# Twelve groups of relayout transfers, handed to the queue three feeds earlier

## The chip, the core and the metric

The kernel runs on one core of a Trainium2 chip. The metric is the device time of one execution in microseconds (us). The engines are TensorE (PE; its weight loads stand apart as PEld), VectorE (DVE), ScalarE (ACT), GpSimd (POOL) and SyncE (SP). SP computes nothing here: it issues most of the DMA transfers, one after the other, from one queue.

## The reference

An RWKV-like recurrence over 768 steps runs for 4 batches of 8 heads of width 40. Its outputs, put side by side per token (3072 tokens of 320 numbers), go through a two-layer feed-forward block with a gate.

```python
for t in range(S):
    y[:, :, t] = np.einsum('bhd,bhde->bhe', rt, state)
    Sa = np.einsum('bhde,bhe->bhd', state, at)
    state_decay = state * wt[:, :, None, :] - np.einsum('bhd,bhe->bhde', Sa, bt)
    state = state_decay + np.einsum('bhd,bhe->bhde', vt, kt)
...
x = np.ascontiguousarray(attn_out.transpose(0, 2, 1, 3)).reshape(B * S, H * D)
h = x @ w_in                       # 320 -> 2048
g = np.where(pos, h, np.where(neg, 0.0, (h + beta) ** 2 / (4.0 * beta)))
return (g @ w_out).astype(np.float32)   # 2048 -> 320
```

## The kernel before, in words

The recurrence is worked in 24 chunks of 32 steps. What a chunk needs is prepared for sets of four chunks at a time, in the background: `prelude` loads w, a, k and b of the next 8 steps from memory (`ld_w`, `ld_a`, `ld_k`, `ld_b`, L258), and ACT copies `ld_w` into the tile `wz` (L267) for two scans on DVE (L235); POOL multiplies (L280, L290, L299) and the rows go out to a scratch tensor (L250). `ab_set` loads rows back from scratch into `lw` and `tiab` (L317); ACT shifts them (L323), DVE transposes them into `ea` (L338) and PE multiplies (L349). `invert` works a triangular inverse on POOL (L376, L382). The chunk itself is `chain`: matmuls L532, L542, L558, L569, L598 with evictions on ACT (L553, L563) and DVE (L576, L600) in between.

A chunk's output lands in the tile `Y` in two roundings: ACT writes the high part (L588) and POOL the low part (L589). Each time two chunks are complete, 64 steps of 4 batches (a token group, 256 columns) are there. `relayout` then copies them by six transfers on SP (L618 three times, L624 twice, L627 once) from `Y` into one of two tiles `X`. The feed-forward block of that group, `moe`, reads `X` in its first matmuls (`ph<-X,w`, L650), gates on ACT, DVE and POOL (L660 to L667) and multiplies again (`po<-w,gh` and `po<-w,gl`, L681). `weights` converts the two weight matrices, in the background too.

All of this is written into one program order, and each engine takes its own instructions in that order. A chunk has four steps; at each, one stage of two chains is written, and then `fill` writes six feeds. A feed (`feed`) writes so many matmuls of `moe` as stand for 1280 columns, then some weight conversion, then `background` some rows of `prelude`, `ab_set` and `invert`. So the transfers that the background issues on SP stand between the six feeds. At the end of the second step of every even chunk, behind the whole fill, stands `relayout`. The feed-forward of a group begins six feeds (7680 columns) behind its relayout: for the first group by the value of `owed`, for the others because a group's work is as many columns as the feeds of two chunks.

A transfer on SP waits for semaphores of the data that it reads and writes. The six of a group wait for the last POOL rounding of `Y` (L589); the matmuls L650 wait for the six; the next roundings of `Y` wait for them too.

Of the kernel before, what the change touches and what calls it, by code (L numbers as in the profile page):

```python
# [44 lines left out]
TRAIL = 2.5  # L45
# [10 lines left out]
def rwkv_moe_kernel(ctx: ExitStack, tc: tile.TileContext, r, k, v, w, a, b, w_in, w_out, ident_d, mask_d, out):  # L56
# [328 lines left out]
    def adopt(s):  # L385

        drain("inv", s)
        W = lw[:, 1024:2048]
        nc.vector.transpose(tinv.rearrange("p c h i -> p i (c h)"), W.rearrange("p (a i) -> p i a", i=32))
        turned_out.add(s)  # L390
# [33 lines left out]
    def background(n):  # L424

        due = []
        for key in ("inv", "ab", "rows"):
            for s in range(1, NS):
                a, b = window(key, s)
                if a < n <= b:  # L430
                    drain(key, s - 1)
                    at = spent.setdefault((key, s), [0])
                    due.append((key, s, at, size[key] * (gone(n) - gone(a)) / (gone(b) - gone(a))))
        while True:
            due = [(k, s, at, to) for k, s, at, to in due if done[k] < s and at[0] < to]
            if not due:
                return
            key, _, at, _ = max(due, key=lambda x: x[3] - x[2][0])
            at[0] += next(back[key])
# [3 lines left out]
    def load_ti(c, hb):  # L443
        drain("rows", c // 4)
        tis[c, hb] = tih[hb]
        load_rows(tih[hb], c, 0, 200, 16 * hb, 16)

    def load_cg(c, hb):
        cg = cgs[(2 * c + hb) % 3]
        hsel = slice(16 * hb, 16 * hb + 16)  # L450
        drain("rows", c // 4)
        sc = scr4[c // 4][c % 4][hsel]
        for f in range(2):
            vr, ur = 64 * (1 - f), 64 * (1 - f) + 32
            nc.sync.dma_start(
                cg[vr : vr + 32, f::2, C_S : C_S + 80], sc[f::2, :, O_V : O_V + 80].rearrange("h t x -> t h x")
            )
            nc.sync.dma_start(
                cg[ur : ur + 32, f::2, C_G : C_G + D], sc[f::2, :, O_B : O_B + D].rearrange("h t x -> t h x")
            )  # L460
# [6 lines left out]
    def shift(c, hb):  # L467
        shift_rows(tis[c, hb])

    def turn(c, hb, part):  # L470
        u = 2 * c + hb
        cg, pr = cgs[u % 3], prs[u % 3]
        t5 = tis[c, hb].rearrange("p h (j x) -> p h j x", x=40)[:, :, :, 0:32]
        if part == 0:
            for f in range(2):
                rows = slice(64 * f, 64 * f + 64)
                nc.vector.transpose(cg[rows, f::2, C_X : C_X + 32], t5[rows, :, 4, :])
        elif part == 1:
            evs[u] = work.tile([128, 8, 2, 32], F32, tag="ev", name="ev")
            nc.vector.transpose(evs[u], t5[:, :, 1:3, :])  # L480
        else:
            nc.vector.transpose(pr[:, :, :, 8:40], t5[:, :, 0:4:3, :])

    def scores(c, hb, parts=(0, 1)):
        u = 2 * c + hb
        for part in parts:
            (score_products, score_masks)[part](u)
# [119 lines left out]
    groups = [(t, 64) for t in range(0, S, 64)]  # L607

    def relayout(g):

        t0, nt = groups[g]
        if g < 2:
            Xt[g] = x_tile(g, F32R)
        X = flat(Xt[g % 2])[0:120, 0 : 24 * nt].rearrange("p (c n) -> p c n", c=6)
        Xb = X.bitcast(F32)
        yf = Y[0].bitcast(F32)[:, :, :, :, t0 % 64 : t0 % 64 + nt]
        for i, (f, p) in enumerate(((0, 0), (1, 0), (0, 2))):
            nc.sync.dma_start(  # L618
                Xb[40 * i : 40 * i + 40, 0:4, :].rearrange("e c (b t) -> e (c b) t", b=NB),
                yf[64 * f : 64 * f + D, p : p + 2].rearrange("e p j b t -> e (p j b) t"),  # L620
            )
        lo = Xb[:, 4:6, :].rearrange("e q (b t) -> e q b t", b=NB)
        for i in range(2):
            nc.sync.dma_start(  # L624
                lo[40 * i : 40 * i + 40], yf[64 : 64 + D, 2 + i, 0].unsqueeze(1).broadcast_to([D, 2, NB, nt])
            )
        nc.sync.dma_start(lo[80:120], yf[64 : 64 + D, 2:4, 1])  # L627
        return X
# [3 lines left out]
    Xs = {}  # L632
# [175 lines left out]
    def pull(gen, n=1):  # L808
        for _ in range(n):
            if next(gen, "end") == "end":  # L810
                return False
        return True
# [50 lines left out]
    def stage(c, hb):  # L863

        if (c, hb) in gens:
            next(gens[c, hb], 0)

    def finish_rounds():

        for f in rounds:  # L870
            f()
        rounds.clear()
# [31 lines left out]
    owed, idle = [0], [True]  # L904
# [7 lines left out]
    def feed(cols):  # L912

        if not Xs:
            return
        owed[0] += cols * (not idle[0])
        while owed[0] > 0:
            d = next(mgen)
            owed[0] = 0 if d is None else owed[0] - d
            idle[0] = d is None  # L920

    def catch_up():

        for f in deferred:
            f()
        deferred.clear()

    def fill():

        catch_up()  # L930
        for k in range(6):
            feed(1280)
            if first:
                first.pop(0)()
            due[0] += PACE
            while due[0] > 0:
                pull(wgen)
                due[0] -= 1
            background(now[0] + 10 / SLOTS * (k + 1) / 6)
        now[0] += 10 / SLOTS  # L940

    for c in range(NC + 1):
        nxt = c + 1 < NC
        if c < NC:
            if c:
                gens[c, 0] = chain(c, 0)
            gens[c, 1] = chain(c, 1)
        stage(c - 1, 1)
        if c:
            stage(c, 0)  # L950
        finish_rounds()
        if c < NC:
            if c and c % 4 == 0:
                adopt(c // 4)
            for j in (0, 1) if c else (2, 0, 1):
                turn(c, 1, j)
        fill()
        stage(c - 1, 1)
        stage(c, 0)
        if nxt:  # L960
            shift(c + 1, 0)
        finish_rounds()
        if c < NC:
            scores(c, 1)
        if nxt:
            load_ti(c + 1, 1)
        if nxt:
            load_cg(c + 1, 0)
            turn(c + 1, 0, 2)
        fill()  # L970
        for g, (t0, nt) in enumerate(groups):
            if t0 + nt == 32 * c:
                Xs[g] = relayout(g)
                if idle[0]:
                    owed[0], idle[0] = -TRAIL * 3072, False
        if c == NC:
            break
        stage(c, 0)
        stage(c, 1)
        finish_rounds()  # L980
        if nxt:
            for j in (0, 1):
                turn(c + 1, 0, j)
        fill()
        stage(c, 0)
        stage(c, 1)
        if nxt:
            shift(c + 1, 1)
        finish_rounds()
        if c + 2 < NC:  # L990
            load_ti(c + 2, 0)
        if nxt:
            scores(c + 1, 0)
            load_cg(c + 1, 1)
            turn(c + 1, 1, 2)
        fill()
# [33 lines left out]
```

## Time and profile before

| | |
|---|---|
| time, median of 3 runs | 774.89 us (773.26 to 779.03) |
| the profiled execution | 778.53 us, of it 776.8 us from its first to its last instruction (the span) |
| busy share of the span: PE, DVE, ACT, POOL | 87%, 76%, 61%, 56% |
| mean granted clock of TensorE | 0.916 of full speed |
| moved by DMA | 102.35 MB, 132 GB/s on the mean |

All starts below are us from the span's first instruction. An engine's row names its line, operation and tiles (`X<-Y`: writes X, reads Y); in square brackets stands how long the engine idled before it and what ended that. Rows of SP are transfers being issued; the length is that of the issue, not of the transfer.

### The profile page before, as it was taken

The numbers are of one execution on the slowest core, as the hardware profiler recorded it, in microseconds if no ns is written. First come the engines' busy times: TensorE is split into PE (matmuls) and PEld (weight loads), VectorE is DVE, ScalarE is ACT, GpSimd is POOL, SyncE is SP. The second block draws the span as 40 slices with busy tenths as digits, with TensorE's granted clock in tenths as the row PEclk, the third lists the DMA queues.
The fourth block names the chain that finished last, engine by engine and source line by source line (L and its number), as shares of the span: only waits on it lengthen the run. The fifth ranks groups of instructions, "written<-read, shape, count | busy, mean of one in ns | idle before, by whom it ended". The sixth has DMA issues, their size and how long they took to land.

```text
span 776.8 us, 35626 instructions
## 1 busy us (share of the span) xinstructions
PE 672.8 (87%) x15360; PEld 620.9 (80%) x15360; DVE 589.2 (76%) x1361; ACT 472.4 (61%) x1016; POOL 433.2 (56%) x603
## 2 busy tenths in 40 slices
PE   4546656796889889899988999999999999999997
PEld 4445546685779778789988889999999999999997
DVE  6999998887769678897788977788777786776211
ACT  5646756775566565565666566665665665655544
POOL 1232999765336998367576486563666732322332
PEclk9865656999699999999999999999999999999999
DMA  8898996998587758684558683443424234330100
GB/s 296 210 218 174 229 204 171 221 211 182 123 183 161 171 133 172 144 191 89 124 115 173 143 171 71 109 80 62 116 47 110 54 71 108 55 89 20 36 20 18
DMA packets 207084, 102.35 MB, mean 132 GB/s; under 512 B 153688, under 2 KB 200792, under 8 KB 206928
## 3 DMA queue, kind: packets, MB, share of 16 engines
q1 hardware_dynamic: 204336, 93.36, 54.2%
q0 software_dynamic: 2432, 6.56, 3.7%
q8 instruction: 121, 1.98, 1.1%
q14 instruction: 35, 0.29, 0.1%
q10 hardware_dynamic: 160, 0.16, 0.1%
HBM read 70.88 MB, written 27.53 MB: 127 GB/s over the span
## 4 chain that ended last, share of the span: by engine, by line
PE 54%; DVE 6%; POOL 4%; DMA 3%; ACT 2%; issue 2%; SPq 2%; POOLq 0%; ACTq 0%; DVEq 0%
PE ph L650 18%; PE po L681 17%; PE p L569 4%; PE p L558 3%; PE p L598 3%; PE p L498 2%; PE p L542 2%; PE p L532 2%; PE p L349 1%; DMA X<-Y 1%; POOL lw L382 1%; POOL lw L376 1%; POOL gl L667 1%; DVE gt L663 1%; DVE wz L235 1%
## 5 line engine op out<-in xcount | busy, mean ns | idle before, releaser
L650 PE MATMUL ph<-X,w 120*128 120x256 f32 x1536 | 219.7, 296 | 6.3 <-DMA X<-Y 5.8
L667 POOL TENSOR_TENSOR gl<-gt,gh 128x512 fp32r<-128x512 f32 x95 | 121.6, 1280 | 162.3 <-ACT gh L666 155.8
L650 PEld LDWEIGHTS ph<-X,w 120*128 120x128 f32 x1536 | 198.0, 198 | 13.9 <-issue 6.0
L681 PE MATMUL po<-w,gh 128*128 128x320 f32 x768 | 136.6, 320 | 4.6 <-ACT gh L666 3.8
L663 DVE SCALAR_TENSOR_TENSOR gt<-gt,ph 128x512 f32<-128x512 f32 x95 | 65.0, 684 | 85.2 <-ACT gt L661 72.8
L681 PEld LDWEIGHTS po<-w,gh 128*128 128x128 f32 x768 | 119.5, 197 | 6.7 <-ACT gh L666 5.0
L666 ACT CAST gh<-gt 128x512 fp32r<-128x512 f32 x95 | 58.8, 619 | 91.7 <-DVE gt L663 84.8
L660 ACT ACTIVATE gt<-ph,half_c 128x512 f32<-128x512 f32 x95 | 65.3, 687 | 54.5 <-PE ph L650 53.7
L382 POOL TENSOR_TENSOR lw<-lw 128x31 f32<-128x31 f32 (+15 forms) x155 | 86.9, 561 | 8.3
L376 POOL TENSOR_TENSOR lw<-lw 128x31 f32<-128x31 f32 (+15 forms) x155 | 85.5, 551 | 8.1
L576 DVE SCALAR_TENSOR_TENSOR cg<-p,pr 40x160 f32<-40x160 f32 x184 | 59.2, 322 | 34.6 <-PE p L569 32.5
L681 PE MATMUL po<-w,gl 128*128 128x320 f32 x384 | 75.8, 320 | 9.5 <-POOL gl L667 9.5
L510 DVE TENSOR_TENSOR cg<-p,mask 32x256 f32<-32x256 f32 x192 | 80.6, 420 | 3.6
L553 ACT ACTIVATE cg<-p 32x160 f32<-32x160 f32 x192 | 56.6, 295 | 30.6 <-DVE cg L549 16.3
L681 PEld LDWEIGHTS po<-w,gl 128*128 128x128 f32 x384 | 62.3, 195 | 11.6 <-POOL gl L667 11.3
L569 PE MATMUL p<-cg 128*64 128x72 f32 (+1 forms) x1536 | 64.0, 241 | 0.0
L549 DVE SCALAR_TENSOR_TENSOR cg<-p,mask 32x128 f32<-32x128 f32 x192 | 55.3, 288 | 11.0 <-ACT cg L553 5.8
L589 POOL TENSOR_TENSOR Y<-yt,Y 128x256 fp32r<-128x256 f32 x48 | 35.7, 744 | 48.5 <-ACT Y L588 48.4
L661 ACT ACTIVATE gt<-gt 128x512 f32<-128x512 f32 x95 | 60.0, 632 | 3.0
L569 PEld LDWEIGHTS p<-cg 128*64 128x64 f32 x1536 | 58.4, 150 | 0.4 <-issue 0.4
L558 PEld LDWEIGHTS p<-cg 128*40 128x40 f32 x1472 | 36.4, 131 | 21.2 <-ACT cg L553 13.1
L558 PE MATMUL p<-cg 128*40 128x40 f32 x1472 | 42.6, 219 | 12.2 <-ACT cg L553 12.2
(105 smaller groups left out, 1085.1 us busy)
## 6 DMA issues: line engine op xcount, KB each, us to landing
ti<-scr SPq DMA_DIRECT2D x96, 200.0 KB
cg<-scr SPq DMA_DIRECT2D x96, 80.0 KB
scr<-arena SPq DMA_DIRECT2D x16, 480.0 KB
X<-Y SPq DMA_DIRECT2D x36, 160.0 KB
scr<-wide SPq DMA_DIRECT2D x8, 640.0 KB
w<-in_moe_w_out_dram SPq DMA_DIRECT2D x16, 320.0 KB
tiab<-scr SPq DMA_DIRECT2D x28, 160.0 KB
cg<-scr SPq DMA_DIRECT2D x96, 40.0 KB
```

What stands on the lines that cost most here:

```text
L376: eng.tensor_mul(t3, W3[:, 0:n, j : j + 1].broadcast_to([128, n, m]), L3[:, j + 1 :, j].unsqueeze(1).broadcast_to([128, n, m]),)
L382: eng.tensor_sub(W3[:, 0:n, j + 1 :], W3[:, 0:n, j + 1 :], t3)
L510: nc.vector.tensor_tensor(out=cg[q, f::2, C_X : C_X + 64][:, 4 * i : 4 * i + 4].rearrange("p h (j x) -> p h j x", x=32), in0=ps[quarter(f, ...
L558: nc.tensor.matmul(pst[er[h % 2], h // 2, :], lhsT=cg[:, h, C_S : C_S + D], rhs=cg[:, h, C_G : C_G + D], start=True, stop=True)
L569: nc.tensor.matmul(psv[h // 8][64 * f : 64 * f + 64, h // 2 % 4, 0:n3], lhsT=cgw[:, h * CW + C_G : h * CW + C_G + 64], rhs=cg[:, h, C_R : ...
L576: nc.vector.scalar_tensor_tensor(out=cn[er[f], f::2, C_S : C_S + D][:, halves[i]], in0=psv[i][er[f], :, 32:72], scalar=-1.0, in1=pr[er[f], ...
L650: nc.tensor.matmul(phs[k % 2][:, n * j : n * j + n], lhsT=wt[0, f // 4, wi // 2][:, wi % 2, fs], rhs=Xs[g][:, xi, :], start=i == 0, stop=i ...
L660: nc.scalar.activation(gt, ph, AF.Relu, bias=half_c, scale=0.5)
L661: nc.scalar.activation(gt, gt, AF.Square)
L663: nc.vector.scalar_tensor_tensor(out=gt, in0=gt, scalar=1.0, in1=ph, op0=ALU.min, op1=ALU.max)
L667: nc.gpsimd.tensor_sub(gl, gt, gh.bitcast(F32))
L681: nc.tensor.matmul(pos[i], lhsT=x[:, ts_], rhs=w, start=q == 0 and k == 0, stop=end)
```

## The change

The call of `relayout` moves from behind the fill of the second step into it, between the third and the fourth of its six feeds. For the first group the value of `owed` is set lower by three feeds, so that the feed-forward begins at the same place as before.

```diff
-    def fill():
+    def fill(midway=()):
 
         catch_up()
         for k in range(6):
+            if k == 3:
+                for f in midway:
+                    f()
             feed(1280)
...
-        fill()
-        for g, (t0, nt) in enumerate(groups):
-            if t0 + nt == 32 * c:
-                Xs[g] = relayout(g)
-                if idle[0]:
-                    owed[0], idle[0] = -TRAIL * 3072, False
+
+        def hand_over():
+
+            for g, (t0, nt) in enumerate(groups):
+                if t0 + nt == 32 * c:
+                    Xs[g] = relayout(g)
+                    if idle[0]:
+                        owed[0], idle[0] = -TRAIL * 3072 - 3 * 1280, False
+
+        fill([hand_over])
```

On PE, DVE, ACT and POOL the instructions stand in the same order as before. On SP the order differs at three of the twelve groups, where the background had issued something in the last three feeds: the first group (chunk 2), the second (chunk 4) and the sixth (chunk 12).

SP at the first group, before:

```order
L752 DMA w_6_1841<-in_moe_w_out_dram 128x640
L258 DMA ld_w<-in_w_dram 128x1x320
L258 DMA ld_a<-in_a_dram 128x1x320
L258 DMA ld_k<-in_k_dram 128x1x320
L618 DMA X_1854<-Y 40x1024 x3
L624 DMA X_1854<-Y 40x2x256 x2
L627 DMA X_1854<-Y 40x2x256
```

And now:

```order
L618 DMA X_1838<-Y 40x1024 x3
L624 DMA X_1838<-Y 40x2x256 x2
L627 DMA X_1838<-Y 40x2x256
L752 DMA w_6_1848<-in_moe_w_out_dram 128x640
L258 DMA ld_w<-in_w_dram 128x1x320
L258 DMA ld_a<-in_a_dram 128x1x320
L258 DMA ld_k<-in_k_dram 128x1x320
```

The six have moved past a load of raw weights and past the three loads of the prelude's next part.

SP at the second group, as a difference:

```order
 L458 DMA cg_86<-scr_106 32x8x40
+L618 DMA X_2931<-Y 40x1024 x3
+L624 DMA X_2931<-Y 40x2x256 x2
+L627 DMA X_2931<-Y 40x2x256
 L258 DMA ld_k<-in_k_dram 128x1x320
 L317 DMA lw<-scr_107 32x16x80 x2
-L618 DMA X_2955<-Y 40x1024 x3
-L624 DMA X_2955<-Y 40x2x256 x2
-L627 DMA X_2955<-Y 40x2x256
 L317 DMA tiab<-scr_107 32x16x80 x2
```

Here they have moved past the load of `ld_k` and the two loads of `lw`.

SP at the sixth group, as a difference:

```order
 L458 DMA cg_87<-scr_108 32x8x40
+L618 DMA X_2931<-Y 40x1024 x3
+L624 DMA X_2931<-Y 40x2x256 x2
+L627 DMA X_2931<-Y 40x2x256
 L250 DMA scr_110<-arena 128x8x40
 L258 DMA ld_k<-in_k_dram 128x1x320
-L618 DMA X_2955<-Y 40x1024 x3
-L624 DMA X_2955<-Y 40x2x256 x2
-L627 DMA X_2955<-Y 40x2x256
```

Here they have moved past one store of rows and one load of `ld_k`.

## Rows read from the trace of the kernel before

**Rows 1.** Busy time by stretch: us, each engine's busy (instructions), clock, DMA share.
```profile
455.00:735.00 280.00, 279.98 (x6340) 262.17 (x6336) 204.40 (x492) 172.50 (x379) 137.95 (x187) 1.00 0.34 75
```

**Rows 2.** Timeline of PE: all waits for X, and one group of equal matmuls without.
```profile
130.14 4.02 PE L650 MATMUL ph<-X,w 120*128 120x256 f32 x16 [2.69 <-DMA X<-Y]
...
439.71 2.17 PE L650 MATMUL ph<-X,w 120*128 120x256 f32 x16
...
447.73 3.36 PE L650 MATMUL ph<-X,w 120*128 120x256 f32 x16 [2.04 <-DMA X<-Y]
...
737.50 0.95 PE L650 MATMUL ph<-X,w 120*128 120x256 f32 x6 [1.08 <-DMA X<-Y]
```

**Rows 3.** Timeline of POOL at the groups: roundings of Y, and two readers of loads.
```profile
123.55 0.72 POOL L589 TENSOR_TENSOR Y<-yt,Y 128x256 fp32r<-128x256 f32 x1
...
130.61 1.31 POOL L280 TENSOR_TENSOR arena<-ld_a,ld_w 128x320 f32<-128x320 f32 x1
...
184.05 0.73 POOL L589 TENSOR_TENSOR Y<-yt,Y 128x256 fp32r<-128x256 f32 x1
...
437.77 0.74 POOL L589 TENSOR_TENSOR Y<-yt,Y 128x256 fp32r<-128x256 f32 x1
...
445.98 1.04 POOL L290 TENSOR_TENSOR arena<-ld_k,wz 128x320 f32<-128x320 f32 x1 [2.65 <-DVE wz L235]
...
731.43 0.74 POOL L589 TENSOR_TENSOR Y<-yt,Y 128x256 fp32r<-128x256 f32 x1
```

**Rows 4.** Timeline of SP at the first group.
```profile
117.25 0.44 SPq L752 DMA_DIRECT2D w<-in_moe_w_out_dram  x1
117.74 0.61 SPq L258 DMA_DIRECT2D ld_w<-in_w_dram  x1
...
124.30 2.87 SPq L618 DMA_DIRECT2D X<-Y  x3
...
128.95 0.77 SPq L627 DMA_DIRECT2D X<-Y  x1
```

**Rows 5.** Timeline of SP at the second group.
```profile
187.00 0.56 SPq L258 DMA_DIRECT2D ld_k<-in_k_dram  x1
188.00 1.68 SPq L317 DMA_DIRECT2D lw<-scr  x2
189.78 2.49 SPq L618 DMA_DIRECT2D X<-Y  x3
...
194.01 0.77 SPq L627 DMA_DIRECT2D X<-Y  x1
```

**Rows 6.** Timeline of SP at the sixth and at the last group.
```profile
439.02 0.41 SPq L250 DMA_DIRECT2D scr<-arena  x1
...
441.21 2.47 SPq L618 DMA_DIRECT2D X<-Y  x3
...
732.20 2.36 SPq L618 DMA_DIRECT2D X<-Y  x3
```

**Rows 7.** Timeline of ACT: what reads the loads that are passed, and follows.
```profile
124.66 0.76 ACT L267 COPY wz<-ld_w 128x320 f32<-128x320 f32 x1
128.02 0.77 ACT L279 COPY arena<-ld_w 128x320 f32<-128x320 f32 x1 [2.60 <-DVE ld_w L235]
...
132.49 0.61 ACT L553 ACTIVATE cg<-p 32x160 f32<-32x160 f32 x2 [1.95 <-DVE cg L549]
...
193.08 0.40 ACT L323 COPY lw<-lw 32x256 f32<-32x256 f32 x1 [2.65 <-DMA lw<-scr]
```

**Rows 8.** Timeline of PE behind these readers.
```profile
134.09 1.12 PE L558 MATMUL p<-cg 128*40 128x40 f32 x32
...
142.20 0.85 PE L681 MATMUL po<-w,gl 128*128 128x320 f32 x4 [2.04 <-POOL gl L667]
...
152.12 1.44 PE L681 MATMUL po<-w,gl 128*128 128x320 f32 x4 [2.28 <-POOL gl L667]
...
195.04 0.67 PE L349 MATMUL p<-ea 40*32 40x32 f32 x32 [4.29 <-DVE ea L338]
```

## The prediction

> **What bounds the kernel now.** I read the page's busy shares first, then the chain of waits, then busy time by stretch, and last the timelines of single engines around the six transfers. From 455 to 735 us PE is busy for 279.98 of 280 us at full clock [rows 1]: that stage is PE's own work, and nothing in a transfer's place can shorten it. Before 455 us PE idles in places, each behind one named wait. The list of who waited for X has three entries, and they are all [rows 2]: 2.69 us before the first group's matmuls at 130.14, 2.04 us at 447.73 (sixth group), 1.08 us at 737.50 (last group), 5.8 us in all. That is everything an earlier X could return directly. The wait also costs clock: sixteen equal matmuls take 2.17 us at 439.71 and 3.36 us behind the wait at 447.73 [rows 2], 1.2 us more.
>
> What do the transfers themselves wait for? Hold the start of L618 on SP against the end of POOL's rounding L589. First group: 123.55 + 0.72 = 124.27 [rows 3], issue at 124.30 [rows 4]. Last group: 731.43 + 0.74 = 732.17 [rows 3], issue at 732.20 [rows 6]. In both, SP already stood at L618 and the rounding released it; a place further ahead in SP's order can't make it earlier. At the second group the rounding ended at 184.78 [rows 3] and the issue came at 189.78 [rows 5]; at the sixth, 438.51 [rows 3] and 441.21 [rows 6]. There SP's own order held the six.
>
> **The change, part by part.** On PE, DVE, ACT and POOL nothing moves. On SP nine of the twelve groups keep their place, since nothing stood between, and I cost them at nothing: same order, same rounding to wait for. This includes the last group, so the 1.08 us at 737.50 stay. Three places differ.
>
> *First group (+6.8 us).* Before, SP issued a weight load at 117.25, `ld_w` at 117.74 and two more loads, and then stood waiting for the rounding until 124.30 [rows 4]. Those loads were out before the wait. Now the six stand ahead of them: SP reaches L618 at 117.2, waits there until 124.3 just the same, issues the six until 128.95 + 0.77 = 129.72 [rows 4], then the weight load (0.44 us), and `ld_w` at about 130.25, issued by 130.9. When does it land? Nearest rows: the three L618 of the last group are issued by 732.20 + 2.36 = 734.56 [rows 6] and PE gets them at 737.50 [rows 2], 2.9 us; the `lw` load issued at 188.00 [rows 5] is there at 193.08 [rows 7], 5.1 us from the start of its issue. So `ld_w` lands between 133.8 and 135.4; I take 134.0, near the short end, because the queue is fresh from a wait. ACT reads it at 124.66 (L267) [rows 7], so ACT stands for 9.4 us (9.1 to 10.7). ACT takes its work in order: behind L267 stands L553 at 132.49, done at 133.10 [rows 7], on which PE's L558 at 134.09 depends [rows 8]. It had 1.0 us to spare, so PE is late by 8.4. POOL is less late. Its L280 needs the scan that ended at 128.02 (ACT's L279 waited for the same) [rows 7] but ran at 130.61, behind POOL's own inverse [rows 3]; 2.6 us of the delay fit there, and POOL is late by 9.4 - 2.6 = 6.8. PE waits for POOL at 142.20, for 2.04 us [rows 8]. There the two delays meet: PE's 8.4 has 2.04 us of idle to eat, POOL's 6.8 sets the end. I take 6.8. The low end lets the second such wait, 2.28 us at 152.12 [rows 8], swallow more: 9.1 - 2.6 - 2.3 = 4.2. The high end lets nothing be swallowed but the 1.0, and adds the slow clock once: 10.7 - 1.0 + 1.2 = 10.9. The first X is not earlier, so its wait stays. The weight load is 12 us late too; its conversion comes after ACT's stop and is hidden under it, without that it would stand where `ld_w` stands now.
>
> *Second group (+4.6 us).* The rounding is long done, so the six go out at 187.0 and take 194.01 + 0.77 - 189.78 = 5.0 us [rows 5]; `ld_k` follows at 192.0 (0.56), `lw` at 192.6 in place of 188.00: 4.6 us later. For `lw` ACT already waits, 2.65 us until 193.08 [rows 7], and behind ACT and DVE PE waits 4.29 us until 195.04 for `ea` [rows 8]. There is no slack on that chain, so the 4.6 us go to the end in full. X of this group comes 2.8 us earlier and nobody was waiting for it. Low end: landing in 2.9 us in place of 5.1, 4.6 - 2.2 = 2.4. High end: the slow clock once more, 5.8.
>
> *Sixth group (-1.2 us).* The six go out at 439.02 in place of 441.21 [rows 6], 2.2 us earlier, more than the wait of 2.04 at 447.73 [rows 2]. So that wait goes, and with it the slow clock: 2.04 + 1.2 = 3.2 us at best. Late next is `ld_k`: behind six transfers of 5.0 us and a store it goes out at 444.5, is issued by 445.1 and lands at 448.0 by the short landing, where POOL's L290 wants it at 445.98 [rows 3]. POOL is 2.0 us late, the low part gl of the gate stands behind it on POOL, and PE needs it in the pass after the one that came forward. 3.2 - 2.0 = 1.2. Ends: -3.2, and +1.0 if `ld_k` lands 2.2 us later still.
>
> Sum: 6.8 + 4.6 - 1.2 = 10.2 us. The profiled execution took 778.53 us, 3.6 us above the median of 774.89; I carry the 10.2 us over to the median: **785.1 us**. The ends add up to +3.4 (4.2 + 2.4 - 3.2) and +17.7 (10.9 + 5.8 + 1.0): 778.3 to 792.6.
>
> A rule speaks for the change, and here it has to be weighed. The Trainium skill, page "DMA: Bandwidth & Descriptors", section "Rules for kernel authors", says to issue a DMA early, compute, and wait for its semaphore late. By it the three waits of PE go and the sum is that of the second rival below. The rows say otherwise for this place: a transfer whose data is not ready is not early, it occupies SP. At the first group SP would stand from 117.2 to 124.3 us with three loads behind it and nothing going out [rows 4].
>
> **The rivals.**
>
> *The delay is swallowed.* Up to 440 us PE has idle time, and a delay of all engines together may free what DMA makes them wait for. For it: the waits for POOL at 142.20 and 152.12. Against it: behind 200 us the engines move in step, and from 455 us on PE has no gap [rows 1]. If half of the two delays goes, (6.8 + 4.6) / 2 - 1.2 = +4.5 us: 779.4 us, within 1%.
>
> *The early issue pays: faster than before.* The place is PE at 130.14, 447.73 and 737.50: all three waits vanish and the clock holds behind each, 5.8 + 3 x 1.2 = 9.4 us: 765.5 us. This is what the rule of the page "DMA: Bandwidth & Descriptors" of the Trainium skill would promise. It decides if the rounding of Y, not SP's order, has the spare time: the six would have to go out well ahead of 124.30 and 732.20. The rows have 0.03 us between rounding and issue, against it. If `ld_w` and `lw` come in time after all (SP would have to be through the six by 124.66 - 2.9 - 0.6 - 0.5 = 120.7 us and by 187.4 us), only the sixth group's 3.2 us are left: 771.7 us, within 1%.
>
> *The change hardly does anything.* Nine of twelve groups don't move on SP. If the three moved loads had slack that I don't see, the time is 774.9. I count this with the swallowed delay.
>
> **How the numbers follow.** A measurement of this kernel tells about 1% (7.7 us) from no change. Forecast, slower by over 1%: 0.64. Delay swallowed or nothing done: 0.23. Only the sixth group's gain: 0.08. Both of these are within 1%: 0.31. The early issue pays, faster by over 1%: 0.05. The range takes the forecast's ends, and goes down to no change for the swallowed delay: 774 to 793 us.
>
> **What would show it.** In the changed kernel's trace: SP's L618 of the first group at 124.3 as before, and `ld_w` at 130, not 117.7; ACT's L267 of that part near 134 with a wait of about 9 us ended by the load; PE's L558 behind it near 142. Some 60 us later ACT's L323 waiting for `lw` by 4 to 5 us more than 2.65. At the sixth group PE's wait for X gone, and POOL's L290 waiting for `ld_k`. The last group's wait for X unchanged at about 1 us. I am wrong if L267 does not wait (then `ld_w` was issued elsewhere), or if PE's L349 of 195.04 stands less than 8 us later than before.

## The result

The changed kernel takes 788.12 us (median of 6 runs, 782.67 to 790.04), the kernel before in the same rounds 779.10 us (median of 6 runs, 773.26 to 780.88). The ratio of changed to before is 1.0123, interval 1.0092 to 1.0155: slower by 7 to 12 us. The forecast was 785.1 us, slower, with a range of 774 to 793. The 3 us between forecast and median come from the base: the forecast stood on a median of 774.89 for the kernel before, 4.2 us below the 779.10 of all rounds. The medians lie 9.0 us apart, where the sum forecast was 10.2. The profiled execution of the changed kernel, the longest of its six, took 790.04 us (span 788.3, mean granted clock 0.900), 11.5 us more than that of before.

### The profile page after: what moved, and what is told of

Same layout as the page of the kernel before. It is cut to its first block, busy times and chain, and to the rows that moved or that the text cites. A ratio compares the mean times of both kernels' runs of the same rounds, so it can differ in the third digit from the quotient of the medians.

```text
span 788.3 us, 35629 instructions
## 1 busy us (share of the span) xinstructions
PE 678.0 (86%) x15360; PEld 625.0 (79%) x15360; DVE 587.8 (75%) x1361; ACT 472.9 (60%) x1016; POOL 433.3 (55%) x603
## 4 chain that ended last, share of the span: by engine, by line
PE 52%; DVE 7%; POOL 4%; DMA 3%; ACT 3%; issue 2%; SPq 1%; POOLq 0%; ACTq 0%; DVEq 0%
PE ph L650 18%; PE po L681 16%; PE p L569 4%; PE p L558 3%; PE p L598 3%; PE p L498 3%; PE p L542 2%; PE p L532 2%; PE p L349 1%; DMA tiab<-scr 1%; POOL lw L382 1%; DVE ld_w L235 1%; POOL lw L376 1%; POOL gl L667 1%; DVE wz L235 1%
## 5 line engine op out<-in xcount | busy, mean ns | idle before, releaser
L650 PE MATMUL ph<-X,w 120*128 120x256 f32 x1536 | 218.7, 296 | 4.2 <-DMA X<-Y 3.8
L667 POOL TENSOR_TENSOR gl<-gt,gh 128x512 fp32r<-128x512 f32 x95 | 121.8, 1282 | 163.9 <-ACT gh L666 156.2
L650 PEld LDWEIGHTS ph<-X,w 120*128 120x128 f32 x1536 | 197.2, 197 | 11.9 <-issue 4.1
L553 ACT ACTIVATE cg<-p 32x160 f32<-32x160 f32 x192 | 56.8, 296 | 32.7 <-DVE cg L549 17.9
L569 PE MATMUL p<-cg 128*64 128x72 f32 (+1 forms) x1536 | 66.5, 246 | 0.0
L589 POOL TENSOR_TENSOR Y<-yt,Y 128x256 fp32r<-128x256 f32 x48 | 35.9, 748 | 49.2 <-ACT Y L588 46.6
L569 PEld LDWEIGHTS p<-cg 128*64 128x64 f32 x1536 | 60.9, 155 | 0.4 <-issue 0.4
L558 PE MATMUL p<-cg 128*40 128x40 f32 x1472 | 43.6, 220 | 17.8 <-ACT cg L553 14.9
L558 PEld LDWEIGHTS p<-cg 128*40 128x40 f32 x1472 | 37.2, 133 | 27.3 <-ACT cg L553 19.0
```

Of the source, the lines that this page charges most:

```text
L558: nc.tensor.matmul(pst[er[h % 2], h // 2, :], lhsT=cg[:, h, C_S : C_S + D], rhs=cg[:, h, C_G : C_G + D], start=True, stop=True)
L569: nc.tensor.matmul(psv[h // 8][64 * f : 64 * f + 64, h // 2 % 4, 0:n3], lhsT=cgw[:, h * CW + C_G : h * CW + C_G + 64], rhs=cg[:, h, C_R : ...
L650: nc.tensor.matmul(phs[k % 2][:, n * j : n * j + n], lhsT=wt[0, f // 4, wi // 2][:, wi % 2, fs], rhs=Xs[g][:, xi, :], start=i == 0, stop=i ...
L667: nc.gpsimd.tensor_sub(gl, gt, gh.bitcast(F32))
```

## The profile after

Where the 11.5 us arose is read best from an event that occurs in both programs at regular places and never moves in its engine's order. POOL's rounding L589 is one: it runs 48 times, twice a chunk. Its starts in both traces:

| what lies between | before, us | after, us | later by |
|---|---|---|---|
| the rounding that the first group waits for | 123.55 | 124.23 | 0.68 |
| the next two | 137.87, 152.02 | 142.76, 158.76 | 4.89, 6.74 |
| before the second group | 184.05 | 191.29 | 7.24 |
| next behind it | 203.72 | 214.00 | 10.28 |
| some 40 us on | 242.39 | 253.46 | 11.07 |
| before the sixth group | 422.03, 437.77 | 432.67, 446.73 | 10.64, 8.96 |
| next behind it | 450.21 | 462.03 | 11.82 |
| before the last group | 731.43 | 742.93 | 11.50 |

So 0.7 us stood there before anything had moved, 6.6 us come with the first group and 3.0 to 3.8 with the second. At the sixth, 1.7 us are won from 422.03 to 437.77 and 2.5 us lost behind it (11.44 us late at the rounding of 463.96). The 1.7 us are not the change's: the kernel with the second group alone (below), whose sixth group stays in its place, wins as much there (1.61 us late, then 0.07 us early). Behind 464 us nothing is lost: PE is busy for 276.77 of the 280 us that answer to [rows 1], and 2.83 us of the rest are one wait of the sixth group, shown further down.

The columns are those of [rows 1]. First the kernel before, at the first group:

```profile
117.00:130.00 13.00, 7.55 (x224) 6.66 (x224) 10.76 (x25) 7.62 (x20) 12.28 (x20) 0.63 0.55 147
130.00:150.00 20.00, 16.46 (x292) 14.79 (x292) 17.64 (x40) 13.20 (x32) 14.73 (x23) 0.88 0.94 221
```

Then the changed kernel:

```profile
117.00:130.00 13.00, 7.20 (x224) 6.33 (x224) 7.92 (x21) 5.29 (x14) 12.35 (x20) 0.63 0.39 96
130.00:150.00 20.00, 13.62 (x232) 12.29 (x236) 14.64 (x33) 10.95 (x25) 12.68 (x20) 0.67 0.75 182
455.00:735.00 280.00, 276.77 (x6312) 258.26 (x6312) 207.35 (x500) 173.36 (x384) 142.22 (x198) 0.99 0.37 81
```

From 117 to 130 us the DMA engines are busy for a share of 0.39 and move 96 GB/s, where the kernel before had 0.55 and 147: the queue holds loads that it does not issue. From 130 to 150 us the granted clock is 0.67 and PE is busy for 13.62 us, before 0.88 and 16.46.

**First group.** SP of the changed kernel, answering to [rows 4]:

```profile
117.44 0.44 SPq L458 DMA_DIRECT2D cg<-scr  x1
124.99 2.51 SPq L618 DMA_DIRECT2D X<-Y  x3
...
130.09 0.49 SPq L752 DMA_DIRECT2D w<-in_moe_w_out_dram  x1
130.62 0.64 SPq L258 DMA_DIRECT2D ld_w<-in_w_dram  x1
```

SP issues nothing from 117.88 to 124.99. An issue's row begins when the waiting is over, so the 7.1 us show as a gap and not as a long row. POOL's rounding ends at 124.23 + 0.73 = 124.96, and the six go 0.03 us later, as before. `ld_w` goes out at 130.62 in place of 117.74. ACT, PE and POOL behind it, one fence for each, answering to [rows 7], [rows 8] and [rows 3]:

```profile
133.72 0.77 ACT L267 COPY wz<-ld_w 128x320 f32<-128x320 f32 x1 [8.27 <-DMA ld_w<-in_w_dram]
135.59 0.77 ACT L279 COPY arena<-ld_w 128x320 f32<-128x320 f32 x1 [1.11 <-DVE ld_w L235]
...
139.90 0.61 ACT L553 ACTIVATE cg<-p 32x160 f32<-32x160 f32 x2 [1.80 <-DVE cg L549]
```

```profile
130.44 4.00 PE L650 MATMUL ph<-X,w 120*128 120x256 f32 x16 [2.30 <-DMA X<-Y]
140.25 1.54 PE L558 MATMUL p<-cg 128*40 128x40 f32 x31 [5.81 <-ACT cg L553]
...
141.66 1.91 PE L569 MATMUL p<-cg 128*64 128x72 f32 x31
...
144.13 2.18 PE L650 MATMUL ph<-X,w 120*128 120x256 f32 x16
...
147.61 0.85 PE L681 MATMUL po<-w,gl 128*128 128x320 f32 x4
...
158.87 1.43 PE L681 MATMUL po<-w,gl 128*128 128x320 f32 x4 [2.83 <-POOL gl L667]
```

```profile
124.23 0.73 POOL L589 TENSOR_TENSOR Y<-yt,Y 128x256 fp32r<-128x256 f32 x1
...
135.64 1.20 POOL L280 TENSOR_TENSOR arena<-ld_a,ld_w 128x320 f32<-128x320 f32 x1 [5.08 <-DVE ld_w L235]
```

One wait of ACT for a load, 8.27 us, turns into 5.81 us of PE idle: PE's wait is put down to ACT's L553, the last of the six rows of ACT behind the late copy, and only ACT's own timeline shows that the cause is a load. The wait for gl at 142.20 [rows 8] is gone (the row at 147.61 has none).

**Second group.** SP and ACT of the changed kernel, answering to [rows 5] and [rows 7]; PE behind them:

```profile
194.52 2.47 SPq L618 DMA_DIRECT2D X<-Y  x3
...
199.54 0.61 SPq L258 DMA_DIRECT2D ld_k<-in_k_dram  x1
200.25 1.06 SPq L317 DMA_DIRECT2D lw<-scr  x2
```

```profile
203.38 0.40 ACT L323 COPY lw<-lw 32x256 f32<-32x256 f32 x1 [5.71 <-DMA lw<-scr]
```

```profile
205.31 0.68 PE L349 MATMUL p<-ea 40*32 40x32 f32 x32 [6.17 <-DVE ea L338]
```

With the 7.24 us that everything is late by here, `lw` goes out 200.25 - 188.00 - 7.24 = 5.0 us later and lands 203.38 - 193.08 - 7.24 = 3.1 us later. PE's L349 stands 10.27 us later than at 195.04 [rows 8], 3.0 of them new.

**Sixth and last group.** SP, POOL and PE of the changed kernel, answering to [rows 6], [rows 3] and [rows 2]:

```profile
448.00 2.47 SPq L618 DMA_DIRECT2D X<-Y  x3
...
453.03 1.41 SPq L250 DMA_DIRECT2D scr<-arena  x1
454.49 0.61 SPq L258 DMA_DIRECT2D ld_k<-in_k_dram  x1
...
743.70 2.35 SPq L618 DMA_DIRECT2D X<-Y  x3
```

```profile
457.80 1.05 POOL L290 TENSOR_TENSOR arena<-ld_k,wz 128x320 f32<-128x320 f32 x1 [5.50 <-DMA ld_k<-in_k_dram]
...
460.08 1.26 POOL L667 TENSOR_TENSOR gl<-gt,gh 128x512 fp32r<-128x512 f32 x1
...
742.93 0.74 POOL L589 TENSOR_TENSOR Y<-yt,Y 128x256 fp32r<-128x256 f32 x1
```

```profile
454.61 0.97 PE L650 MATMUL ph<-X,w 120*128 120x256 f32 x6
455.96 1.43 PE L650 MATMUL ph<-X,w 120*128 120x256 f32 x10 [0.38 <-DMA X<-Y]
...
461.40 1.43 PE L681 MATMUL po<-w,gl 128*128 128x320 f32 x4 [2.83 <-POOL gl L667]
462.76 1.30 PE L558 MATMUL p<-cg 128*40 128x40 f32 x32
463.85 2.17 PE L569 MATMUL p<-cg 128*64 128x72 f32 x32
...
749.00 0.96 PE L650 MATMUL ph<-X,w 120*128 120x256 f32 x6 [1.09 <-DMA X<-Y]
```

PE's wait for X falls from 2.04 [rows 2] to 0.38 us, and in its place stands one of 2.83 us for gl. That gl is POOL's L667 at 460.08, which stands behind L290 and its `ld_k`. The last group's wait is 1.09 us in place of 1.08 [rows 2].

## The experiments

The theory: the six, moved ahead of loads in SP's order, hold these loads up, by a wait for the rounding (first group) or by their own 5 us of issue (second, sixth). The rivals: it is the extra traffic of the transfers at an earlier time; or the loss is spread over the program and not at the three places. Every ratio is to the kernel before, in the same rounds.

**One group at a time.** `relayout` is called in the middle for the named group alone, at the end for the others.

```diff
+            if t0 + nt == 32 * c and (g in (0,)) == early:
...
+        fill([lambda: hand_over(True)])
+        hand_over(False)
```

> Only the first group's six transfers are handed out midway, the other eleven at the end of the fill. Queue theory (what a place costs is set by the loads that stand behind the six on SP, and the places add up): about +6.6 us (ratio 1.0085), ACT's L267 waiting some 8 us for ld_w, and at the second group ACT's wait for lw near the 2.65 us of before. Rival (the loss is one of the second group, and what the first loses is swallowed by waits that follow): within 2 us of before. Rival (the whole 11.5 us come from the first group): 1.015.

Measured: ratio 1.0122 (1.0084 to 1.0159), 786.64 us against 777.31, from only 5 runs. ACT of this kernel:

```profile
132.92 0.75 ACT L267 COPY wz<-ld_w 128x320 f32<-128x320 f32 x1 [8.75 <-DMA ld_w<-in_w_dram]
```

The second group's `lw` is waited for by 2.42 us, as before. The first group's wait and its place are shown. The size is less clean: by the starts of L589 some 6 us arise at the group, and 3.7 us more between 323 and 349 us, where this kernel moves nothing. In the other traces that stretch takes from 0.1 us less to 2.3 us more than in the kernel before, so most of the 3.7 us may be chance. By the profile the group's own share is then 6 us, a little below what the ratio's interval (6.5 to 12.4 us) holds.

```diff
+            if t0 + nt == 32 * c and (g in (1,)) == early:
```

> Only the second group's six go out midway. Queue theory: no wait at L267 of the first group, ACT's wait for lw at the second group 5 to 6 us in place of 2.65, and +3 to +4.6 us in all (ratio 1.004 to 1.006). Rival (the second group only loses because the first has shifted it): no change, ratio 1.000. Rival (the landing of lw is set by the traffic of the transfers in flight, not by the place on SP): the wait stays near 2.65 and the time with it.

Measured: 1.0046 (1.0015 to 1.0078), 779.73 us against 777.31. ACT of this kernel:

```profile
194.52 0.40 ACT L323 COPY lw<-lw 32x256 f32<-32x256 f32 x1 [6.00 <-DMA lw<-scr]
```

No wait for `ld_w` at the first group. The second group costs 1 to 6 us by itself, and where it was said to.

```diff
+            if t0 + nt == 32 * c and (g in (5,)) == early:
```

> Only the sixth group's six go out midway. The prediction's term: PE's wait for X of 2.04 us goes, POOL waits for ld_k, net -1.2 us (ratio 0.9985). From the changed kernel's trace: X's wait under 0.5 us, POOL's L290 waiting some 5 us for ld_k and PE some 2.8 us for gl behind it, so that nothing is won or up to 2.5 us lost (ratio 1.000 to 1.003). Rival (the wait for X is the cost and ld_k has slack): -3.2 us, 0.996.

Measured: 1.0017 (0.9991 to 1.0044), 778.50 us against 777.31. Its PE has no wait for X left there, but one for gl, as the changed kernel has:

```profile
445.91 2.17 PE L650 MATMUL ph<-X,w 120*128 120x256 f32 x16
...
451.84 0.85 PE L681 MATMUL po<-w,gl 128*128 128x320 f32 x4 [2.58 <-POOL gl L667]
452.62 1.24 PE L558 MATMUL p<-cg 128*40 128x40 f32 x32
453.64 2.17 PE L569 MATMUL p<-cg 128*64 128x72 f32 x32
```

Behind this wait the granted clock was 0.52 from 452.6 to 455.8 us. A gain of 1.2 us, as the prediction had it (about 0.9985), lies just outside the interval. The wait was exchanged, not removed.

```diff
+            if t0 + nt == 32 * c and (g in (1, 2, 3, 4, 5, 6, 7, 8, 9, 10, 11)) == early:
```

> All groups but the first hand their six out midway, so that on SP the second and the sixth group's orders are those of the changed kernel and the first group's that of before. It tells whether the places add up: e2 and e3 alone gave 1.0046 and 1.0017, e1 alone 1.0122, the whole change 1.0123. If they add up: 1.004 to 1.007, ACT's wait for lw near 6 us. Rival (once the first group's delay is there the others cost nothing, alone they cost more): 1.006 to 1.010 here. Rival (the second group costs only together with the first): 1.000 to 1.002.

Measured: 1.0050 (1.0017 to 1.0083), 783.58 us against 778.93. ACT waits 5.66 us for `lw`, as expected. The ratio is what the second and the sixth add up to (1.0046 and 1.0017), so the nine groups that keep their place on SP cost nothing that shows. By the starts of L589 the second group costs 3.0 us (0.11 us late before it, 3.07 behind it) and the sixth nothing (3.43, then 3.26). PE at the sixth group has the same wait for gl, but the granted clock behind it is 1.00 (456.1 to 458.5 us):

```profile
455.34 0.85 PE L681 MATMUL po<-w,gl 128*128 128x320 f32 x4 [2.58 <-POOL gl L667]
456.13 0.81 PE L558 MATMUL p<-cg 128*40 128x40 f32 x32
456.76 1.20 PE L569 MATMUL p<-cg 128*64 128x72 f32 x32
```

With the first group's 1.0122 it gives 1.0172, against 1.0123 for the whole; the difference of 0.005 lies within the joint uncertainty of the three, about 0.006. So whether parts of the delays overlap is not decided.

**Three early, three late.** The first three transfers of every group in the middle of the fill, the last three at its end. SP's wait for the rounding stays; the issue ahead of the loads is shorter by 2.5 us.

```diff
-        lo = Xb[:, 4:6, :].rearrange("e q (b t) -> e q b t", b=NB)
+        def rest():
+            lo = Xb[:, 4:6, :].rearrange("e q (b t) -> e q b t", b=NB)
...
+        later.append(rest)
...
+        fill([hand_over])
+        while later:
+            later.pop()()
```

> The first three of the six (L618) go out midway, the last three at the end of the fill, in all groups. It halves the six's own issue ahead of the loads (2.5 of 5 us) and leaves the wait for the rounding of Y ahead of them (7 us at the first group, none at the second). Queue theory: L267's wait falls from 8.3 by 2.5 to some 5.8 us, lw's wait at the second group from 5.7 to near 3.5; +5 to +8 us in all (ratio 1.006 to 1.010). Rival (only the wait for the rounding counts): first group as in the changed kernel, +6.6, second group nothing. Rival (only the issue of the six counts): half of the changed kernel's loss at both, +5.5 us, with L267's wait near 4.

Measured: 1.0085 (1.0053 to 1.0117), 783.56 us against 777.31. ACT of this kernel:

```profile
131.95 0.76 ACT L267 COPY wz<-ld_w 128x320 f32<-128x320 f32 x1 [6.49 <-DMA ld_w<-in_w_dram]
```

The wait for `ld_w` went from 8.27 to 6.49 us, by less than the 2.5 us of issue taken out of its way. At the second group `lw` was issued at 193.72, earlier against the six than in the changed kernel, and still waited for by 5.54 us, since it took 5.4 us to land; that half of the expectation failed. A shorter queue ahead of `ld_w` shortens its wait, as the theory has it, and the landing is a term of its own. That the time gains by it is not shown: the interval overlaps that of the whole change (1.0092 to 1.0155).

**The second group one feed later than before.** The six of this group alone go out behind the first feed of the third step's fill. If traffic right behind `lw` makes it land late, moving the six further back should help.

```diff
+            if k == 1:
+                for f in midway:
+                    f()
...
+                if t0 + nt == 32 * c and (g in (1,)) == late:
...
-        fill()
+        fill([lambda: hand_over(True)])
```

> The other way round: the kernel before, with the second group's six handed out one feed later, so that on SP only the two loads of tiab change places with them; the lw loads no longer have the six right behind them. So far lw landed 5.0 us after its issue where the six follow (before, e1, e3, e4) and 3.1 us where they don't (changed kernel, e2). If the traffic right behind a load holds it up: lw lands in 3.1 us, ACT's wait for it falls from 2.65 to under 1 us, PE's for ea by as much, and about -2 us in all (ratio 0.9975). Rival (place on SP alone counts; the difference in landing came from something else): lw lands in 5 us, ratio 1.000.

Measured: 0.9993 (0.9963 to 1.0023), 777.12 us against 777.40. `lw` was issued at 188.73 and landed at 193.56, 4.8 us, with the six behind the next loads (`tiab`):

```profile
193.56 0.40 ACT L323 COPY lw<-lw 32x256 f32<-32x256 f32 x1 [2.33 <-DMA lw<-scr]
```

The expected gain did not come: traffic right behind the load is not what holds it. Traffic ahead of the loads does not hold them either: in the changed kernel `ld_w` landed 133.72 - 130.62 = 3.1 us after its issue and `lw` 203.38 - 200.25 = 3.1 us, sooner than the 5.1 us of `lw` before. So the rival of the extra traffic falls at these two places; what came late is the issue.

**The first group's rounding made earlier.** In the first of three, the first group is early as above, and the one rounding that it waits for (chunk 1, second half) runs on DVE and not on POOL. Then SP has almost nothing to stand for at the same place in its order, and the wait for `ld_w` should shrink with it.

```diff
-            nc.gpsimd.tensor_sub(yv[:, 1], yt, yv[:, 0].bitcast(F32))
+            (nc.vector if (c, hb) == (1, 1) else nc.gpsimd).tensor_sub(yv[:, 1], yt, yv[:, 0].bitcast(F32))
...
+            if t0 + nt == 32 * c and (g in (0,)) == early:
```

> As e1 (only the first group's six go out midway), and the one rounding that they wait for is made by DVE in place of POOL, where it stood behind the inverse; it should be done near 119.5 us in place of 124.3. Queue theory (SP stands for the rounding with the loads behind it): the six go out 4 to 5 us earlier, so does ld_w, L267 waits 3 to 4 us in place of 8.75, and of e1's loss 4 us come back: +2 to +5 us against before (ratio 1.003 to 1.006). Rival (the loss is the six's own issue and traffic ahead of the loads): L267's wait and the time as in e1 (ratio 1.012).

Measured: 1.0030 (1.0000 to 1.0059), 779.24 us against 777.40. SP and ACT of this kernel:

```profile
118.10 2.52 SPq L618 DMA_DIRECT2D X<-Y  x3
...
123.77 1.41 SPq L258 DMA_DIRECT2D ld_w<-in_w_dram  x1
```

```profile
127.23 0.78 ACT L267 COPY wz<-ld_w 128x320 f32<-128x320 f32 x1 [4.10 <-DMA ld_w<-in_w_dram]
```

Same order on SP, same transfers, less waiting in the queue: the six go at 118.10 and not at 123.71 as in the kernel with the first group alone (0.6 us of that stood there before), ACT's wait halves, and the ratio falls from 1.0122 to 1.0030. That is the theory's strongest evidence. The wait that is left, 4.10 us, fits the six's own issue of 5.1 us ahead of the load. The ratio fell by 7 us and the wait by 4.65; with the two intervals the fall is 3 to 11 us.

The control: the kernel before with that rounding on DVE and nothing else.

```diff
+            (nc.vector if (c, hb) == (1, 1) else nc.gpsimd).tensor_sub(yv[:, 1], yt, yv[:, 0].bitcast(F32))
```

> The control of e6: the kernel before with that one rounding on DVE. The six of the first group go out once the three loads are issued, near 120.3 us in place of 124.3, and PE's wait for X at 130 us shrinks or goes; ACT and DVE bound the stage there, so little of it reaches the end: -2 to +1 us (ratio 0.998 to 1.001). Rival (the first X is on the path): -3 us or more.

Measured: 0.9988 (0.9960 to 1.0016), 776.60 us against 777.40. The six go at 120.06, 4.2 us earlier than in [rows 4], behind the loads, and PE's wait for X at 130.14 [rows 2] is gone:

```profile
127.87 3.78 PE L650 MATMUL ph<-X,w 120*128 120x256 f32 x16
133.74 1.54 PE L558 MATMUL p<-cg 128*40 128x40 f32 x31 [2.09 <-ACT cg L553]
```

PE began on X 2.3 us earlier and met ACT's L553 0.35 us earlier than the 134.09 of [rows 8]. So the largest of the three waits for X was never worth its 2.69 us: another wait stood right behind it. With the first group early as well (the kernel ahead of this one), the wait for L553 is 3.68 us long and PE begins at 133.79. At the rounding of 111.41, ahead of all changes, that execution was 1.24 us early and the control 0.30 us late, so it is some 1.6 us behind the control here.

The third has the first and the last group's rounding on DVE, on top of the kernel before; the hope was a version faster than both.

```diff
+            (nc.vector if (c, hb) in ((1, 1), (NC - 1, 1)) else nc.gpsimd).tensor_sub(yv[:, 1], yt, yv[:, 0].bitcast(F32))
```

> The kernel before, with the roundings that release the first and the last group's six made by DVE in place of POOL, the order on SP as before. It takes away what the six wait for, where the change only moved the six ahead of other transfers. Last group: the rounding stands behind POOL's gl today (731.43, behind a 1.29 us pass from 730.19); DVE is idle there, so the six go out some 1 us earlier, PE's wait of 1.08 us goes and the slow clock behind it with it, -1.5 to -2.5 us; first group as in e7, -1 to 0 us. In all -1.5 to -3.5 us, ratio 0.996 to 0.998, and faster than both kernels if it holds. Rival (the landing of the six, not the rounding, sets PE's wait): ratio as in e7, 0.999, with PE still waiting 1 us.

Measured: 0.9996 (0.9968 to 1.0023), 778.73 us against 778.93. PE at the last group:

```profile
739.47 0.95 PE L650 MATMUL ph<-X,w 120*128 120x256 f32 x6 [0.80 <-DMA X<-Y]
```

The wait went from 1.08 to 0.80 us only, since DVE's pass took 1.31 us (below). The gain of 1.5 to 3.5 us that was expected did not come, and no version tried is shown to be faster than the kernel before.

## Why the prediction was right, and where not

*What bounds the kernel, and what releases the six: right.* From 464 us on nothing is lost (11.44 us late at the rounding of 463.96, 11.50 at the last). At the first and the last group the six still go 0.03 us behind the rounding.

*Nine groups at nothing, the last one among them: right,* by the starts of L589 and by the kernel without the first group.

*First group, +6.8: the size right (6.6), the path different.* `ld_w` landed at 133.72 (134.0 forecast), and the wait was 8.27 us, where 9.4 were forecast: the load came 0.3 us sooner, and ACT reached it 0.8 us later than before. POOL was taken to set the end, with 6.8 us. POOL's L280 is only 135.64 - 130.61 - 0.68 = 4.4 us late: the step from ACT's copy to DVE's scan, for which L279 waited 2.60 us [rows 7], now takes 1.11: DVE stood idle for 7.42 us before that scan, where in the kernel before it was busy with other passes until 126.40. PE set the end. Behind its 5.81 us of idle the clock fell (L558 took 1.54 us in place of 1.12 [rows 8], L569 1.91), and its next L650, at 144.13, stands 6.7 us late net of the 0.68. It ate the 2.04 us wait of [rows 8], as foreseen, and then lost 2 us again: the waits for ACT and POOL in the next pass were longer by 0.8 and 0.55 us, and the clock fell behind them. Two errors, a POOL term too large and a second round of waits left out, cancelled.

The rule on issuing a transfer early (the Trainium skill, "DMA: Bandwidth & Descriptors", "Rules for kernel authors") is borne out at one of three places: the wait for X shrank by 1.7 us at the sixth group, where SP's order had held the six, by 0.4 us at the first and not at the last. At the first group, issued early in program order, the six went at the same moment as before, and what stood behind them paid.

*Second group, +4.6: the mechanism right, the size at its low side, 3.0 to 3.8.* The issue is 5.0 us later (4.6 forecast). The landing took 3.1 us from the issue and not 5.1. That was the low end's case (2.9 us, +2.4). The wait grew by 3.1 us (4 to 5 forecast), and L349 stands 10.3 us later in all (at least 8 forecast).

*Sixth group, -1.2: this step failed; no gain is shown.* What was foreseen came: the wait for X went, `ld_k` came late and POOL with it. But "POOL is 2.0 us late" was subtracted as 2.0 us. POOL's L290 ran 2.9 us late against the rounding ahead of it (457.80 - 445.98 - 8.96), part of it a store that took 1.41 in place of 0.41 us to issue, and the new wait of PE for gl is 2.83 us. It cost clock as the old one had: L558 and L569 took 1.30 and 2.17 us behind it, 0.81 and 1.20 at full clock. The clock's price was charged to the wait that goes and forgotten for the one that comes. The size of the term stays open. From PE's L542 ahead of the X wait to its L650 behind the gl wait, the kernel before takes 11.5 us and the changed kernel 13.8, which is +2.3. The kernel with the sixth group alone takes 12.0 (+0.5) and the one with all groups but the first 10.8 (-0.7), with a wait for gl of 2.58 us in both. Six kernels whose sixth group stays in its place take 11.05 to 11.92. The ratio of the sixth group alone, 1.0017, holds -0.7 to +3.4 us.

*The sum is close in part by luck.* In the two profiled executions the second group was taken too large by 0.8 to 1.6 us and the sixth too small by 3.5, and 1.7 us that are not the change's were won from 422 to 438 us.

*The rivals of the prediction.* The delay was not swallowed: that case was 4.5 us, a ratio of 1.006, and the interval begins at 1.0092. The early issue did not pay.

## What to carry to other kernels

Before a transfer is moved forward in a queue that issues in order, look for what releases it: if its issue follows the end of its producer by hundredths of a us, its place is not what holds it, and each load behind it pays for the time that it now blocks the queue. List those loads and follow each to its first reader, then to whoever stands behind that reader on its engine; the wait appears there under another name. Charge a new wait the same clock price that is credited for the one removed, and charge it as a range: here the same wait was followed once by half clock and once by full clock.

## What was not expected of the hardware

**Landing of `lw`.** The same load took 5.1 us from issue to reader in the kernel before, 4.8 and 5.4 us in two experiments, and 3.1 us in the changed kernel, with the second group alone and with all groups but the first. In these three the whole six went out ahead of it; in the others they went behind it, at once, split or one pair of loads later. What sets it stays open.

**DVE beside POOL.** The rounding took 0.65 us on DVE at the first group and 1.31 us at the last. DVE and POOL of the control, and then of the kernel with two roundings:

```profile
118.92 0.65 DVE L589 TENSOR_TENSOR Y<-yt,Y 128x256 fp32r<-128x256 f32 x1 [1.27 <-ACT Y L588]
```

```profile
118.59 0.70 POOL L382 TENSOR_TENSOR lw<-lw 128x240 f32<-128x240 f32 x1
```

```profile
732.70 1.31 DVE L589 TENSOR_TENSOR Y<-yt,Y 128x256 fp32r<-128x256 f32 x1 [1.05 <-ACT Y L588]
```

```profile
732.44 1.29 POOL L667 TENSOR_TENSOR gl<-gt,gh 128x512 fp32r<-128x512 f32 x1 [3.58 <-ACT gh L666]
```

Both times DVE ends 0.28 us after the POOL pass that had begun before it (119.57 and 119.29; 734.01 and 733.73). The Trainium skill, page "SBUF — State Buffer", section "SBUF: two separate sides", says that a DVE instruction with two inputs in SBUF (Y and yt are such tiles) and a GpSimd instruction that reads SBUF exclude each other for a whole instruction. Two places agree with that; no run here has the same rounding on DVE with POOL idle.

**The clock behind a wait.** Behind the wait of 2.58 us for gl, L569 took 2.17 us with the sixth group alone (granted clock 0.52) and 1.20 us in the kernel with all groups but the first (1.00): the same wait, once followed by half clock and once not. A clock price per wait is then a size that differs between executions by a microsecond or more.
